# One core, attention over memories and an erf-softplus FFN: smaller TensorE bundles, one tile for both halves of the activation, a planner margin and a new order

## The chip, the cores and the metric

The kernel runs on one core of one Trainium2 chip. The metric is device time in microseconds, median over runs. Beside the runs, one execution was taken by the hardware profiler; all rows below come from that one.

## The reference

Eight batches of eight heads, 576 positions, head size 64, 32 memory slots, all in float32:

```python
a = softmax(phi, axis=positions)                # phi: B,H,576,32
k_m, v_m = a^T k, a^T v                         # 32 x 64 for each head
attn = softmax(q k_m^T / 8)                     # 576 x 32
x = concat over heads of attn v_m               # 4608 x 512
h = x w_in                                      # 512 -> 2048
out = (h * erf(softplus(h))) w_out              # 2048 -> 512
```

## The kernel before, in words

**The algebra.** Nothing is multiplied by `x`. For each batch the kernel builds `v_m w_in` ("vw", 256 rows of 32 slots by 8 heads, `vw`, L802), so the first FFN product is attention weights times vw (`psh`). Most products are made exact enough by splitting each float32 operand into a rounded half and a remainder (`hi`, `lo`) and adding three products: hi by hi, hi by lo, lo by hi (`products`, L1008). From batch 2 on the first product uses seven block products instead of eight (`ffn1_pair`, L958), on blocks that `at_blocks` (L927) makes. After it come, for each of the 128 steps (8 batches by 16 column blocks of 128), softplus and erf on ACT (L1066, L1071) and `g_split` (L1074) on DVE: `e*h` (L1097), a cast to `g_hi` (L1099), a subtraction to `g_lo` (L1100). POOL copies the last 64 positions of each half into `rest` (L1104). `ffn2` (L1114) multiplies `g_hi`, `g_lo` by the weights `wo` into four PSUM banks `pso0` to `pso3`; `ffn2_rest` (L1137) does the 64 left over positions of two batches at once into `psr`. Steps 0 to 5 use whole float32 operands (`i < FR2`).

**Small products.** Three kinds of product use only parts of the TensorE array: the sums over positions that give `k_m`, `v_m` (`sums_and_turn`, L668, tiles of 128x32, 64x32 or 116x32), the scores (`attention`, L877, 64x32, 16 matmuls) and vw (`vw`, L802, 64x32, 32 matmuls for four column blocks). They are emitted in bundles by `together` (L632). The first operation of a bundle claims every tile that the bundle writes, thus all its PSUM banks at once: two for scores, two for sums from batch 2 on, two for vw. The pool `ps` has four banks, which `psh` and `psr` use too. `PARTS` (L1282 to L1293) says which pieces go in one bundle: each batch has four vw bundles; from batch 2 on one also takes the next batch's sums, and two (in batch 2 three) also take scores of the next batch. That is 16 shared bundles of four banks each (five with sums, eleven with scores).

**The order.** Every piece of work is an `Op` with a rank (lower is earlier), a cost and the engines that may do it. `Plan.order` (L133) runs a small model of the engines once, at build time, and emits the instructions in that order. At each turn an engine takes the lowest rank among what is ready within 100 ns (L174). TensorE, when it has just run a small operation and another small one is ready, takes that one (L169). A change from large to small products is charged `SWITCH`, 98 ns, and one back `SWITCH + RELOAD`, 213 ns (L208). What an operation writes counts as ready `SIGNAL`, 60 ns, after its end (L237). The costs are in `mm`, `on_dve`, `on_act` (L349 to L356). Where TensorE would be idle for over 450 ns before the first `ffn2`, `fill` (L384) puts in matmuls of the identity. `WHEN` (L296) holds the ranks of the pieces; at the end a table (L1346) adds a number to the rank of some 400 operations, and another (L1399) fixes the engine of some 50.

**Buffers.** `AB` = 9 tiles for the attention blocks (a batch from 2 on needs 7), `WB` = 3 tiles `win`: two hold the blocks of `w_in` that `win_again` (L466) brings back from memory for one vw bundle, and `vraw`, an intermediate of `vw_sums` (L837), takes the third. `g_hi` and `g_lo` have three tiles each. SP issues nearly all DMAs.

Of the kernel before, what the change touches and what calls it, by code (L numbers as in the profile page):

```python
# [76 lines left out]
class Plan:  # L77
# [8 lines left out]
    AHEAD, WORTH = 0.0, 0.4  # L86

# [45 lines left out]
    def order(self):  # L133
# [11 lines left out]
        releases, out, now, held = [], [], 0.0, set()  # L145

# [16 lines left out]
        while len(out) < len(self.ops):  # L163
# [70 lines left out]
            for y in x.after:  # L234
                n_wait[y] -= 1
                same = e == PE and PE in y.ways
                y.ready = max(y.ready, free[PE] if same else x.end + self.SIGNAL)  # L237
                if not n_wait[y]:
                    for w in y.ways:
                        waiting[w].append(y)  # L240
            for k in x.tiles:
                if k in left:
                    left[k] -= 1
                    if not left[k]:
                        end = max(u.end for u in self.users[k]) + self.SIGNAL
                        heapq.heappush(releases, (end, len(out) * 16 + len(releases), self.pool_of[k]))
# [4 lines left out]
def tile_memory_attention_then_erf_softplus_ffn(  # L251
# [11 lines left out]
    nc = tc.nc  # L263
# [21 lines left out]
    HB, EB, AB, WB, SB, QB = 6, 5, 9, 3, 3, 0  # L285
# [10 lines left out]
    WHEN = dict(phiT=-27.5, phi=-31.75, phi_sums=-20.75, kv=-21, kv_step=-3.0, q0=-12.0, q1=-9.25, sums=-20.25, turn=-12.5, numbers=-19.0, turned=-13, part0=-3, part1=1, part2=5, part3=8.5, win=-2.25, at=-1, p0=0, p1=0.26, p2=-4.45, p3=0.31, p4=-3.9, p5=0.65, p6=-1.05, copy=-40, g=-1.25, ffn2=0.5, soft=2.05, erf=4.35, put=0, put2=1.25, vws=4.01)  # L296
# [23 lines left out]
    room.update({"g_hi": 3, "g_lo": 3, "raw": RAW, "ps": 4, "sc": SB, "dk": 1, "bias": 1, "phiT": 2, "row": 2})  # L320
# [28 lines left out]
    def mm(n, exact):  # L349
        return 2 * (2 * n / 2.4 + 2.5) if exact else n / 2.4 + (15.5 if n == DM else 11.7)  # L350
# [723 lines left out]
    def g_split(rank, i):  # L1074
# [3 lines left out]
        if i < FR2:  # L1078
            t = tile_(("g_hi", "g_lo")[i % 2], "g", i, shape=[P, S], pool="g")
            if i < IN_PSUM:  # L1080
                for x, (half, ps) in enumerate(halves_of(i)):
                    op(DVE, on_dve(U), rank, [(e, x), ps], [(t, x)],
                       lambda half=half, ps=ps: nc.vector.tensor_tensor(
                           out=get(t)[:, half], in0=get(e)[:, half], in1=get(ps)[:, :U], op=ALU.mult))
            else:
                op(DVE, on_dve(S), rank, [e, h], [t], lambda: nc.vector.tensor_tensor(
                    out=get(t), in0=get(e), in1=get(h), op=ALU.mult))
            part = [(("rest", k, x), b % 2) for x in range(2)]
            op(POOL, 400, rank, [t], part[:1], lambda: nc.gpsimd.tensor_copy(
                out=rest[:, k, 0, cols], in_=get(t)[:, NT * P :]))  # L1090
            op(POOL, 400, rank, [t, part[0]], part[1:], lambda: nc.gpsimd.tensor_tensor(
                out=rest[:, k, 1, cols], in0=get(t)[:, NT * P :],
                in1=rest[:, k, 0, cols].bitcast(F32), op=ALU.subtract))
            return
        hi = tile_("g_hi", "g_hi", i, shape=[P, S], dtype=F32R, pool="g")
        lo = tile_("g_lo", "g_lo", i, shape=[P, S], dtype=F32R, pool="g")
        op(DVE, on_dve(S), rank, [e, h], [e], lambda: nc.vector.tensor_tensor(  # L1097
            out=get(e), in0=get(e), in1=get(h), op=ALU.mult))
        op(DVE, on_dve(S, 1), rank, [e], [hi], lambda: nc.vector.tensor_copy(out=get(hi), in_=get(e)))  # L1099
        op(DVE, on_dve(S), rank, [e, hi], [lo], lambda: nc.vector.tensor_tensor(  # L1100
            out=get(lo), in0=get(e), in1=get(hi).bitcast(F32), op=ALU.subtract))
        for x, y in enumerate((hi, lo)):
            op(POOL, 400, rank, [y], [(("rest", k, x), b % 2)],
               lambda x=x, y=y: nc.gpsimd.tensor_copy(out=rest[:, k, x, cols], in_=get(y)[:, NT * P :]))  # L1104
# [9 lines left out]
    def ffn2(rank, i, d):  # L1114
# [5 lines left out]
        gs = [("g", i)] if exact else [("g_hi", i), ("g_lo", i)]  # L1120
# [6 lines left out]
        def emit():  # L1127
            w = [wf[k // 2][:, k % 2]] if exact else [get(w_key)[:, x, k % 2] for x in range(2)]
            matmuls(get(o), products([get(t)[:, d * P : (d + 1) * P] for t in gs], w), k == 0,
# [25 lines left out]
    def last_block(rank, i, gs, w_key):  # L1155
# [10 lines left out]
        for x in range(2):  # L1166
            def emit(x=x):
                matmuls(get(y[x]), products(
                    [get(g)[:, d] for g in gs], [get(w_key)[:, z, k % 2, x * n : (x + 1) * n] for z in range(2)]),
                    k == NK - TAIL, k == NK - 1)  # L1170
# [114 lines left out]
    for b in range(1, B):  # L1285
# [4 lines left out]
        for q in range(b == 1, 4):  # L1290
            PARTS.append((o + WHEN[f"part{q}"], more[q] + [(vw, b, 4 * q)]))
# [54 lines left out]
    for n, d in {  # L1346
# [139 lines left out]
```

## Time and profile before

| | |
|---|---|
| Median of the runs shown | 697.7 us (lowest 696.26) |
| The profiled execution's own time | 695.43 us |
| Its span, first to last instruction | 693.6 us |
| Instructions | 13481 |
| Moved from and to HBM | 86.50 MB read, 17.83 MB written |

The profiler lists matmuls (PE) and weight loads (PEld) apart. A matmul's listed end is modelled and runs into the next one, so the distance from start to start says what one costs, and the "busy" share of PE says little about how close it is to its best.

### The profile page before, as it was taken

To read this page: it belongs to the slowest core of one execution; us is meant where nothing else is said; L and a number is where in the kernel's file an instruction comes from. 1 tells how busy PE (TensorE), PEld (TensorE's weight loads), DVE (VectorE), ACT (ScalarE), POOL (GpSimd) and SP (SyncE) were. 2 spreads that over 40 slices of the span, in tenths; PEclk is the share of its full clock that TensorE was granted. 3 is DMA by queue.
4 is the path that set the end of the run, shared out by engine and by line. 5 is a ranking of instruction groups with operands and counts; after the bars stand their busy time and mean duration, and the time that the engine had idled before them with its cause. 6 is when DMAs were issued, how large, how long until landed. Compare 5 with 4: busy or idle time off the path is not lost.

```text
span 693.6 us, 13481 instructions
## 1 busy us (share of the span) xinstructions
PE 684.2 (99%) x5159; PEld 547.9 (79%) x5159; DVE 585.8 (84%) x1141; ACT 495.4 (71%) x813; POOL 133.4 (19%) x262
## 2 busy tenths in 40 slices
PE   8999999999999999999999999999999999999998
PEld 4566588888888877877888887888888878888886
DVE  4999999787968999999986799999976799978362
ACT  4799977979565886787674886587854677767461
POOL 0020375122102111211110123221311111211020
PEclk9999999999999999999999999999999999999999
DMA  9999950686225443354016633642112331120002
GB/s 363 416 407 402 414 188 32 198 288 188 100 80 200 174 134 120 162 191 160 1 9 241 200 69 112 243 151 108 62 47 84 91 107 61 62 92 32 0 1 76
DMA packets 29792, 105.20 MB, mean 152 GB/s; under 512 B 4000, under 2 KB 4896, under 8 KB 29728
## 3 DMA queue, kind: packets, MB, share of 16 engines
q1 hardware_dynamic: 29296, 103.27, 41.1%
q10 hardware_dynamic: 432, 1.08, 0.4%
q8 instruction: 40, 0.66, 0.4%
q14 instruction: 24, 0.20, 0.1%
HBM read 86.50 MB, written 17.83 MB: 150 GB/s over the span
## 4 chain that ended last, share of the span: by engine, by line
PE 79%; DVE 9%; ACT 5%; DMA 5%; issue 2%; SPq 0%; POOL 0%; ACTq 0%; DVEq 0%; POOLq 0%
PE pso L1109 44%; PE psh L1109 18%; PE psr L1109 6%; PE psa L794 5%; PE psh L1031 4%; PE psa L703 2%; DMA q<-qT 2%; DMA win<-w_in_away 1%; DMA out<-ot 1%; DVE g_lo L1100 1%; DVE e L1097 1%; DVE w L486 1%; DVE g_hi L1099 1%; ACT e L1066 1%; DVE h L989 1%
## 5 line engine op out<-in xcount | busy, mean ns | idle before, releaser
L1109 PE MATMUL pso<-wo,g_hi 128*128 128x512 f32 x970 | 304.9, 395 | 0.8 <-ACT ot L1186 0.8
L1109 PEld LDWEIGHTS pso<-wo,g_hi 128*128 128x128 f32 x970 | 170.3, 188 | 34.1 <-issue 6.4
L1109 PE MATMUL pso<-wo,g_lo 128*128 128x512 f32 x485 | 189.5, 391 | 0.0
L1104 POOL CAST rest<-g_hi 128x64 fp32r<-128x64 f32 x122 | 70.6, 582 | 407.4 <-DVE g_hi L1099 379.7
L1109 PE MATMUL psh<-at,vw_hi 128*128 128x288 f32 x672 | 143.4, 302 | 0.3 <-DVE h L984 0.2
L1109 PEld LDWEIGHTS psh<-at,vw_hi 128*128 128x128 f32 x672 | 113.7, 188 | 24.7 <-ACT h L985 7.1
L985 ACT ACTIVATE h<-psh 128x288 f32<-128x288 f32 x130 | 53.2, 411 | 80.3 <-PE psh L1109 79.5
L1109 PEld LDWEIGHTS pso<-wo,g_lo 128*128 128x128 f32 x485 | 91.1, 188 | 20.7 <-DVE g_lo L1100 0.2
L1097 DVE TENSOR_TENSOR e<-e,h 128x576 f32<-128x576 f32 x122 | 90.2, 752 | 11.3 <-ACT e L1071 11.0
L1066 ACT ACTIVATE e<-h 128x576 f32<-128x576 f32 x127 | 84.2, 681 | 21.4 <-DVE h L989 14.4
L1109 PE MATMUL psh<-at,vw_lo 128*128 128x288 f32 x336 | 99.2, 295 | 0.0
L1100 DVE TENSOR_TENSOR g_lo<-e,g_hi 128x576 fp32r<-128x576 f32 x122 | 92.3, 761 | 2.7
L989 DVE TENSOR_TENSOR h<-psh,h 128x288 f32<-128x288 f32 x144 | 64.0, 452 | 26.0 <-ACT h L985 14.0
L1071 ACT ACTIVATE e<-e 128x576 f32<-128x576 f32 x128 | 81.9, 679 | 0.4
L1104 POOL CAST rest<-g_lo 128x64 fp32r<-128x64 f32 x122 | 59.1, 487 | 84.7 <-DVE g_lo L1100 76.6
L1109 PEld LDWEIGHTS psh<-at,vw_lo 128*128 128x128 f32 x336 | 63.3, 188 | 0.3 <-DVE vw_lo L873 0.3
L1099 DVE CAST g_hi<-e 128x576 fp32r<-128x576 f32 x122 | 54.5, 453 | 7.9 <-PE pso L1109 7.0
L1109 PE MATMUL psr<-wo,rest 128*128 128x512 f32 x192 | 47.6, 392 | 0.0
L1071 ACT ACT_TABLE_LOAD x33 | 42.3, 1283 | 0.6
L1066 ACT ACT_TABLE_LOAD x32 | 41.1, 1283 | 0.6
L1109 PEld LDWEIGHTS psr<-wo,rest 128*128 128x128 f32 x192 | 35.3, 188 | 7.7 <-issue 0.8
L984 DVE COPY h<-psh 128x288 f32<-128x288 f32 x62 | 27.9, 450 | 7.6 <-PE psh L1109 7.2
(116 smaller groups left out, 871.9 us busy)
## 6 DMA issues: line engine op xcount, KB each, us to landing
win<-w_in_away SPq DMA_DIRECT2D x56, 512.0 KB, 5.3
kv<-kv SPq DMA_DIRECT2D x31, 640.0 KB, 7.0
q<-qT SPq DMA_DIRECT2D x16, 576.0 KB, 7.6
w<-w_in SPq DMA_DIRECT2D x8, 1023.8 KB, 14.6
w<-w_out SPq DMA_DIRECT2D x8, 1023.8 KB, 14.8
out<-ot SPq DMA_DIRECT2D x31, 256.0 KB, 2.4
w_in_away<-win SPq DMA_DIRECT2D x12, 512.0 KB, 5.4
phi<-phi SPq DMA_DIRECT2D x7, 640.0 KB, 4.7
```

What stands on the lines that cost most here:

```text
L794: nc.tensor.matmul(out=get(ps[par])[p * M : (p + 1) * M, first:n], lhsT=w[rows, p, :], rhs=x_of(rows, p), start=True, stop=True,)
L984: lambda: nc.vector.tensor_copy(out=to(), in_=get(ps[bank])),
L985: other={ACT: (on_act(U, True), lambda: nc.scalar.activation(to(), get(ps[bank]), AF.Identity))})
L989: op(DVE, on_dve(U), rank + 100 * WHEN["copy"], [ps[bank], key], [key], lambda: nc.vector.tensor_tensor(out=to(), in0=get(ps[bank]), in1=t ...
L1031: nc.tensor.matmul(out=get(ps)[:, :U], lhsT=x[:, g, k % 4 * P : (k % 4 + 1) * P], rhs=y[:, g, :], start=(n + g == 0), stop=(n == len(parts ...
L1066: last[:] = [op(ACT, on_act(S), rank, [("h", i)], [e], lambda: nc.scalar.activation(get(e), get(("h", i)), AF.Softplus), kind="softplus", ...
L1071: last[:] = [op(ACT, on_act(S), rank, [e], [e], lambda: nc.scalar.activation(get(e), get(e), AF.Erf), kind="erf", edge=edge, after=last)]
L1097: op(DVE, on_dve(S), rank, [e, h], [e], lambda: nc.vector.tensor_tensor(out=get(e), in0=get(e), in1=get(h), op=ALU.mult))
L1099: op(DVE, on_dve(S, 1), rank, [e], [hi], lambda: nc.vector.tensor_copy(out=get(hi), in_=get(e)))
L1100: op(DVE, on_dve(S), rank, [e, hi], [lo], lambda: nc.vector.tensor_tensor(out=get(lo), in0=get(e), in1=get(hi).bitcast(F32), op=ALU.subtract))
L1104: lambda x=x, y=y: nc.gpsimd.tensor_copy(out=rest[:, k, x, cols], in_=get(y)[:, NT * P :]))
L1109: nc.tensor.matmul(out=o, lhsT=y, rhs=z, start=(start and n == 0), stop=(stop and n == len(parts) - 1), skip_group_check=again,)
```

## The change

- `PARTS`: from batch 2 on, sums and scores leave the vw bundles. Each of them becomes a bundle of its own, with two banks, at the rank of the vw bundle plus `WHEN["apart"]` = -1 step. Batches 0 and 1 keep theirs.
- `g_split`: one tile `g` of [128, 2, 576] holds both halves (room 3), under two keys; steps 0 to 5 share one tile for two steps. POOL copies both halves' last 64 positions with one instruction after `lo`, in place of one each. The cast to the hi half may go to ACT, where the planner finds that earlier.
- The planner: an operation that TensorE may run counts an operand from another engine as ready `LEAD` = 120 ns later, and a buffer whose first user is on TensorE comes free 120 ns later. TensorE costs rise by 1.5 ns (512 columns) and 0.5 ns (288 columns).
- Buffers: `AB` 9 to 8, `WB` 3 to 4.
- `WHEN`, the table of rank offsets and the table of fixed engines are new throughout.

```diff
+    LEAD = 120.0
...
+        first = {p: min(self.users[ks[0]], key=self.ops.index) for p, ks in self.turn.items() if self.users[ks[0]]}
+        by_pe = {p for p, x in first.items() if PE in x.ways}
...
-                y.ready = max(y.ready, free[PE] if same else x.end + self.SIGNAL)
+                lead = self.LEAD if PE in y.ways else 0.0
+                y.ready = max(y.ready, free[PE] if same else x.end + self.SIGNAL + lead)
...
+                        end += self.LEAD if self.pool_of[k] in by_pe else 0.0
...
-    HB, EB, AB, WB, SB, QB = 6, 5, 9, 3, 3, 0
+    HB, EB, AB, WB, SB, QB = 6, 5, 8, 4, 3, 0
...
-    room.update({"g_hi": 3, "g_lo": 3, "raw": RAW, "ps": 4, "sc": SB, "dk": 1, "bias": 1, "phiT": 2, "row": 2})
+    room.update({"g": 3, "raw": RAW, "ps": 4, "sc": SB, "dk": 1, "bias": 1, "phiT": 2, "row": 2})
...
-        return 2 * (2 * n / 2.4 + 2.5) if exact else n / 2.4 + (15.5 if n == DM else 11.7)
+        return 2 * (2 * n / 2.4 + 2.5) if exact else n / 2.4 + (17.0 if n == DM else 12.2)
...
-        hi = tile_("g_hi", "g_hi", i, shape=[P, S], dtype=F32R, pool="g")
-        lo = tile_("g_lo", "g_lo", i, shape=[P, S], dtype=F32R, pool="g")
+        t = tile_("g", "g", i, shape=[P, 2, S], dtype=F32R, pool="g")
+        hi, lo = g_keys(i)
...
-        op(DVE, on_dve(S, 1), rank, [e], [hi], lambda: nc.vector.tensor_copy(out=get(hi), in_=get(e)))
+        op(DVE, on_dve(S, 1) + 65, rank, [e], [hi], lambda: nc.vector.tensor_copy(out=get(t)[:, 0], in_=get(e)),
+           other={ACT: (on_act(S), lambda: nc.scalar.activation(get(t)[:, 0], get(e), AF.Identity))})
...
-        for x, y in enumerate((hi, lo)):
-            op(POOL, 400, rank, [y], [(("rest", k, x), b % 2)],
-               lambda x=x, y=y: nc.gpsimd.tensor_copy(out=rest[:, k, x, cols], in_=get(y)[:, NT * P :]))
+        op(POOL, 600, rank, [hi, lo], [(("rest", k, x), b % 2) for x in range(2)],
+           lambda: nc.gpsimd.tensor_copy(out=rest[:, k, :, cols], in_=get(t)[:, :, NT * P :]))
+
+    def g_keys(i):
+        return [(("g", i - i % 2), i % 2)] if i < FR2 else [(("g", i), x) for x in range(2)]
...
-            PARTS.append((o + WHEN[f"part{q}"], more[q] + [(vw, b, 4 * q)]))
+            n = o + WHEN[f"part{q}"]
+            if b == 1:
+                PARTS.append((n, more[q] + [(vw, b, 4 * q)]))
+            else:
+                PARTS.append((n, [(vw, b, 4 * q)]))
+                PARTS += [(n + WHEN["apart"], [f]) for f in more[q]]
```

## Rows read from the trace of the kernel before

**Rows 1.** The page, part 1: busy us (share of the span) xinstructions.

```profile
PE 684.2 (99%) x5159; PEld 547.9 (79%) x5159; DVE 585.8 (84%) x1141; ACT 495.4 (71%) x813; POOL 133.4 (19%) x262
```

**Rows 2.** TensorE by lines, 47.5 us to the end: xcount | busy us, mean ns | idle.

```profile
L1109 PE MATMUL pso<-wo,g_hi 128*128 128x512 f32 x970 | 304.9, 395 | 0.8 <-ACT ot L1186 0.8
L1109 PE MATMUL pso<-wo,g_lo 128*128 128x512 f32 x485 | 189.5, 391 | 0.0
L1109 PE MATMUL psh<-at,vw_hi 128*128 128x288 f32 x672 | 143.4, 302 | 0.3 <-DVE h L984 0.2
L1109 PE MATMUL psh<-at,vw_lo 128*128 128x288 f32 x336 | 99.2, 295 | 0.0
L1109 PE MATMUL psr<-wo,rest 128*128 128x512 f32 x192 | 47.6, 392 | 0.0
L794 PE MATMUL psa<-win,kvm 64*32 64x256 f32 x960 | 32.9, 379 | 1.2 <-DMA win<-w_in_away 1.2
L1031 PE MATMUL psh<-at_hi,vw_hi 128*128 128x288 f32 x96 | 21.2, 303 | 0.0
...
L703 PE MATMUL psa<-kv,phi 128*32 128x128 f32 (+1 forms) x560 | 16.8, 276 | 0.5 <-ACT phi L597 0.5
L1109 PE MATMUL pso<-w,g 128*128 128x512 f32 x32 | 15.0, 602 | 0.0
```

**Rows 3.** The chain that ended last, 180 to 366 us: start us, us, what.

```profile
187.17 7.50 PE pso L1109 x33
...
300.40 1.19 PE psh L1109 x9
```

**Rows 4.** TensorE timeline, a shared bundle: start us, us, engine line op tiles xcount.

```profile
311.59 0.39 PE L1109 MATMUL pso<-wo,g_lo 128*128 128x512 f32 x1
311.91 0.71 PE L794 MATMUL psa<-q,kvm 64*32 64x288 f32 x16
312.42 1.07 PE L794 MATMUL psa<-win,kvm 64*32 64x256 f32 x32
313.42 0.73 PE L1109 MATMUL pso<-wo,g_hi 128*128 128x512 f32 x2
313.99 0.39 PE L1109 MATMUL pso<-wo,g_lo 128*128 128x512 f32 x1
```

**Rows 5.** TensorE timeline, a bundle of vw alone.

```profile
322.81 1.09 PE L794 MATMUL psa<-win,kvm 64*32 64x256 f32 x32
323.84 0.53 PE L1109 MATMUL psh<-at,vw_hi 128*128 128x288 f32 x2
```

**Rows 6.** TensorE timeline, scores alone (batch 1, first of two).

```profile
57.14 0.71 PE L794 MATMUL psa<-q,kvm 64*32 64x288 f32 x16
57.79 1.13 PE L1109 MATMUL pso<-w,g 128*128 128x512 f32 x2
```

**Rows 7.** Waits of the weight loads: us in total, times, longest us.

```profile
PEld psh L1109 <- ACT h L985: 7.1, 27, 0.5
```

**Rows 8.** Timeline at 418 us, vw waiting for its weights.

```profile
418.01 0.67 PE L794 MATMUL psa<-win,kvm 64*32 64x256 f32 x16 [0.71 <-DMA win<-w_in_away]
...
419.20 0.67 PE L794 MATMUL psa<-win,kvm 64*32 64x256 f32 x16 [0.52 <-DMA win<-w_in_away]
```

**Rows 9.** TensorE by lines, whole span: the filling matmuls.

```profile
L390 PE MATMUL idle<-ident 128*128 128x512 f32 (+3 forms) x44 | 20.8, 599 | 1.4 <-POOL ident masks.py:199 1.4
```

**Rows 10.** DVE and ACT by lines: the cast to g_hi, a whole-width activation.

```profile
L1099 DVE CAST g_hi<-e 128x576 fp32r<-128x576 f32 x122 | 54.5, 453 | 7.9 <-PE pso L1109 7.0
L1066 ACT ACTIVATE e<-h 128x576 f32<-128x576 f32 x127 | 84.2, 681 | 21.4 <-DVE h L989 14.4 <-DVE g_lo L1100 4.5 <-DVE h L1048 1.5
```

**Rows 11.** Timeline, change from batch 2 to 3: second early block, last tile, products.

```profile
242.75 0.43 ACT L941 ACTIVATE at<-f 128x288 fp32r<-128x288 f32 x1
...
268.26 1.18 DVE L943 TENSOR_TENSOR at<-f,at 128x288 fp32r<-128x288 f32 x3
...
273.06 0.53 PE L1109 MATMUL psh<-at,vw_hi 128*128 128x288 f32 x2
```

More of the change, by code (lines that the diff above doesn't have):

```diff
@@ L295, in tile_memory_attention_then_erf_softplus_ffn @@
     IN_PSUM = 1
-    WHEN = dict(phiT=-27.5, phi=-31.75, phi_sums=-20.75, kv=-21, kv_step=-3.0, q0=-12.0, q1=-9.25, sums=-20.25, turn=-12.5, numbers=-19.0, turned=-13, part0=-3, part1=1, part2=5, part3=8.5, win=-2.25, at=-1, p0=0, p1=0.26, p2=-4.45, p3=0.31, p4=-3.9, p5=0.65, p6=-1.05, copy=-40, g=-1.25, ffn2=0.5, soft=2.05, erf=4.35, put=0, put2=1.25, vws=4.01)
+    WHEN = dict(phiT=-32.0, phi=-32.75, phi_sums=-20.75, kv=-21, kv_step=-3.0, q0=-14.75, q1=-10.25, sums=-21.25, turn=-14.5, numbers=-17.25, turned=-14.25, part0=-3, part1=1, part2=5.25, part3=9.0, win=-2.25, at=-1.25, p0=0, p1=0.76, p2=-4.2, p3=0.31, p4=-1.9, p5=0.9, p6=0.95, copy=-40, g=-2.25, ffn2=0.5, soft=6.05, erf=4.35, put=-0.25, put2=1.25, vws=2.51, apart=-1)
     TAIL = 3
@@ L1078, in g_split @@
         if i < FR2:
-            t = tile_(("g_hi", "g_lo")[i % 2], "g", i, shape=[P, S], pool="g")
+            if i % 2 == 0:
+                tile_("g", "g", i, shape=[P, 2, S], pool="g")
+            t, of = g_keys(i)[0], lambda: g_of(i)[0]
             if i < IN_PSUM:
                 for x, (half, ps) in enumerate(halves_of(i)):
-                    op(DVE, on_dve(U), rank, [(e, x), ps], [(t, x)],
+                    op(DVE, on_dve(U), rank, [(e, x), ps], [t],
                        lambda half=half, ps=ps: nc.vector.tensor_tensor(
-                           out=get(t)[:, half], in0=get(e)[:, half], in1=get(ps)[:, :U], op=ALU.mult))
+                           out=of()[:, half], in0=get(e)[:, half], in1=get(ps)[:, :U], op=ALU.mult))
@@ L1085, in g_split @@
             else:
                 op(DVE, on_dve(S), rank, [e, h], [t], lambda: nc.vector.tensor_tensor(
-                    out=get(t), in0=get(e), in1=get(h), op=ALU.mult))
+                    out=of(), in0=get(e), in1=get(h), op=ALU.mult))
             part = [(("rest", k, x), b % 2) for x in range(2)]
             op(POOL, 400, rank, [t], part[:1], lambda: nc.gpsimd.tensor_copy(
-                out=rest[:, k, 0, cols], in_=get(t)[:, NT * P :]))
+                out=rest[:, k, 0, cols], in_=of()[:, NT * P :]))
@@ L1091, in g_split @@
             op(POOL, 400, rank, [t, part[0]], part[1:], lambda: nc.gpsimd.tensor_tensor(
-                out=rest[:, k, 1, cols], in0=get(t)[:, NT * P :],
+                out=rest[:, k, 1, cols], in0=of()[:, NT * P :],
                 in1=rest[:, k, 0, cols].bitcast(F32), op=ALU.subtract))
             return
-        hi = tile_("g_hi", "g_hi", i, shape=[P, S], dtype=F32R, pool="g")
-        lo = tile_("g_lo", "g_lo", i, shape=[P, S], dtype=F32R, pool="g")
+        t = tile_("g", "g", i, shape=[P, 2, S], dtype=F32R, pool="g")
@@ L1097, in g_split @@
+        hi, lo = g_keys(i)
         op(DVE, on_dve(S), rank, [e, h], [e], lambda: nc.vector.tensor_tensor(
             out=get(e), in0=get(e), in1=get(h), op=ALU.mult))
-        op(DVE, on_dve(S, 1), rank, [e], [hi], lambda: nc.vector.tensor_copy(out=get(hi), in_=get(e)))
+        op(DVE, on_dve(S, 1) + 65, rank, [e], [hi], lambda: nc.vector.tensor_copy(out=get(t)[:, 0], in_=get(e)),
+           other={ACT: (on_act(S), lambda: nc.scalar.activation(get(t)[:, 0], get(e), AF.Identity))})
         op(DVE, on_dve(S), rank, [e, hi], [lo], lambda: nc.vector.tensor_tensor(
-            out=get(lo), in0=get(e), in1=get(hi).bitcast(F32), op=ALU.subtract))
@@ L1102, in g_split @@
-        for x, y in enumerate((hi, lo)):
-            op(POOL, 400, rank, [y], [(("rest", k, x), b % 2)],
-               lambda x=x, y=y: nc.gpsimd.tensor_copy(out=rest[:, k, x, cols], in_=get(y)[:, NT * P :]))
+            out=get(t)[:, 1], in0=get(e), in1=get(t)[:, 0].bitcast(F32), op=ALU.subtract))
+        op(POOL, 600, rank, [hi, lo], [(("rest", k, x), b % 2) for x in range(2)],
+           lambda: nc.gpsimd.tensor_copy(out=rest[:, k, :, cols], in_=get(t)[:, :, NT * P :]))
+    def g_keys(i):
+        return [(("g", i - i % 2), i % 2)] if i < FR2 else [(("g", i), x) for x in range(2)]
@@ L1106, in matmuls, with g_of @@
+    def g_of(i):
+        return [get(("g", i - i % 2))[:, i % 2]] if i < FR2 else [get(("g", i))[:, x] for x in range(2)]
     def matmuls(o, parts, start, stop, again=False):
@@ L1119, in ffn2 @@
             tile_(f"pso{d}", *o)
-        gs = [("g", i)] if exact else [("g_hi", i), ("g_lo", i)]
+        gs = g_keys(i)
         w_key = raw_of[k // 2] if exact else wo[k // 2]
@@ L1128, in emit @@
             w = [wf[k // 2][:, k % 2]] if exact else [get(w_key)[:, x, k % 2] for x in range(2)]
-            matmuls(get(o), products([get(t)[:, d * P : (d + 1) * P] for t in gs], w), k == 0,
+            matmuls(get(o), products([t[:, d * P : (d + 1) * P] for t in g_of(i)], w), k == 0,
                     k == NK - 1 - TAIL * ((b, d) == (B - 1, NT - 1)))
@@ L1168, in emit @@
                 matmuls(get(y[x]), products(
-                    [get(g)[:, d] for g in gs], [get(w_key)[:, z, k % 2, x * n : (x + 1) * n] for z in range(2)]),
+                    [g[:, d] for g in g_of(i)], [get(w_key)[:, z, k % 2, x * n : (x + 1) * n] for z in range(2)]),
                     k == NK - TAIL, k == NK - 1)
@@ L1399, in tile_memory_attention_then_erf_softplus_ffn @@
     for n, e in {
-        45: ACT, 46: ACT, 104: DVE, 174: ACT, 212: ACT, 233: ACT, 326: DVE, 479: DVE, 481: ACT, 503: ACT,
-        576: DVE, 597: DVE, 710: ACT, 779: DVE, 782: ACT, 814: ACT, 850: DVE, 920: DVE, 1249: DVE, 1513: ACT,
-        1516: DVE, 1633: DVE, 1641: DVE, 1643: DVE, 1669: DVE, 1672: ACT, 1675: ACT, 1816: ACT, 1998: DVE,
-        2100: DVE, 2145: DVE, 2198: DVE, 2241: ACT, 2272: DVE, 2484: DVE, 2492: DVE, 2516: DVE, 2571: DVE,
-        2698: DVE, 2729: DVE, 2733: ACT, 2762: DVE, 2785: DVE, 2795: DVE, 2835: ACT, 2857: ACT, 2877: DVE,
-        2906: ACT, 2960: DVE, 3128: ACT,
+        210: DVE, 262: ACT, 290: DVE, 299: ACT, 301: ACT, 324: ACT, 368: ACT, 416: ACT, 420: ACT, 464: DVE,
+        473: DVE, 495: ACT, 520: ACT, 548: ACT, 615: ACT, 665: DVE, 742: DVE, 857: DVE, 902: DVE, 918: DVE,
+        989: DVE, 1064: ACT, 1072: ACT, 1113: ACT, 1120: ACT, 1164: DVE, 1176: DVE, 1256: DVE, 1280: ACT,
+        1290: ACT, 1351: ACT, 1368: DVE, 1375: DVE, 1383: ACT, 1461: DVE, 1497: ACT, 1557: DVE, 1582: DVE,
+        1619: DVE, 1622: DVE, 1673: DVE, 1711: DVE, 1787: DVE, 1825: DVE, 1876: DVE, 1956: ACT, 1972: DVE,
+        1981: ACT, 1989: ACT, 1995: ACT, 2088: ACT, 2091: ACT, 2197: ACT, 2202: ACT, 2229: ACT, 2280: DVE,
+        2363: ACT, 2437: ACT, 2447: DVE, 2511: ACT, 2604: DVE, 2635: DVE, 2689: ACT, 2737: DVE, 2741: DVE,
+        2770: DVE, 2774: ACT, 2795: ACT, 2813: DVE, 2840: ACT, 2860: ACT, 2916: ACT, 3027: DVE, 3030: DVE,
     }.items():
```

107 rows, old and new, of the table g are left out of this document.

## The prediction

> **What bounds the kernel now.** I read the page's busy shares first, then TensorE by lines, then the chain for undisturbed pitches, then the timeline around bundles, then the waits. The page says that TensorE (PE) is busy for 99% of the span, DVE for 84%, ACT for 71% [rows 1]. Since a matmul's listed end is modelled, the 99% cannot say how much of PE's time is waiting. The pitch can: 33 matmuls of 512 columns in a row take 7.50 us, 227.3 ns each, and nine of 288 columns 1.19 us, 132.2 ns each [rows 3].
>
> From 47.5 us to the end, 646.1 us, PE's own work is then worked out from the counts [rows 2]:
>
> - 512 columns, split operands: 970 + 485 + 192 = 1647 at 227.3 ns: 374.3 us
> - 288 columns: 672 + 336 + 3 x 96 (one of three equal rows stands there) = 1296 at 132.2 ns: 171.4 us
> - whole float32 operands: 32 take 15.0 us; the code has 16 more alike: 22.5 us in all
> - small products: vw 32.9, sums 16.8, and 14 lots of scores at 57.79 - 57.14 = 0.65 us [rows 6], 9.1: 58.8 us
> - the last 18 half-width matmuls, at half of 227 ns: 2 us
>
> That is 629.0 us, so waits, changes between large and small products, and the last store hold only 17 us. Before 47.5 us PE does little: 20.8 us go to filling matmuls [rows 9], put there because inputs and decoded weights are not there yet.
>
> So PE's own work is the bound. The change alters none of the counts of full-array matmuls. It can gain only from those 17 us and from the filled first stretch, and it can lose by adding changes between product kinds. To be faster by over 2% (about what a measurement of this kernel can tell from no change), 14 us, it would have to take nearly all the waiting out.
>
> **The change part by part.**
>
> *Bundles of their own.* In the shared bundle the scores begin 311.91 - 311.59 = 0.32 us after the last large matmul, 0.09 over the pitch; the bundle lasts 313.42 - 311.91 = 1.51 us; the two matmuls behind it take 0.57 us, 0.115 over two pitches [rows 4]. vw alone lasts 1.03 us [rows 5] and scores alone 0.65 [rows 6], together 1.68, or 0.17 more than shared. A split that stands apart therefore costs 0.17 + 0.09 + 0.115 = 0.375 us of PE. Sums I price alike. There are 16 of them: 6.0 us if every one stands apart, nothing where the planner runs the two back to back, which it does when the second is ready as the first ends. A gain in this term itself is excluded, since no small product goes away. With the scores ranked one step ahead they often will be apart, but new rank offsets may undo that; I take six of 16, +2.25 us. What it buys is room: two PSUM banks are claimed at a time, not all four, so the pool need not be empty before a bundle. The trace shows no long wait ahead of the bundle above (0.09 us), so the room buys less waiting behind it at most.
>
> The Trainium skill has a rule that speaks against this edit. In "TensorEngine Tiling (Array Packing)", section "Tiling Modes", key properties, it says that changing the tiling mode, not just the tile, drains TensorE. The trace agrees in kind: the change in and out costs the 0.09 and 0.115 us above. By the rule alone every separate bundle pays, the 6.0 us; by the row it is paid only where a large matmul comes between.
>
> *Margin for TensorE's operands.* Weight loads for the first product waited 27 times for ACT's copy out of `psh`, 7.1 us in total [rows 7], 0.26 us each. Part of that is hidden by the matmul under way. Of the 17 us about 6 to 7 are changes into and out of some thirty bundles at 0.205 us; the other 10 hold the last store too, and I count 7 of them as waits. A planner that counts operands as ready later puts other work in front of such a product. Ends: all 7 gone, or as many new ones since the whole order is new, +7; I take a third, -2.5 us. It costs nothing where `ffn2` work lies ready, and six steps of lag keep some.
>
> *Fourth `win` buffer.* One vw bundle waited for its weights, 0.71 and 0.52 us of idle PE [rows 8]. Two blocks and `vraw` fill the three buffers, so the next blocks start late. The fourth lets one block of the two start earlier. Ends 0 and -1.2; I take -1.0, as the new order also moves the loads. It is part of the 7.
>
> *One tile `g`, one POOL copy, cast on either engine.* POOL loses 122 instructions at 19% busy [rows 1], off every long wait of PE; its copy now waits for `lo`, but `rest` is needed only for `psr`, a batch later. The cast takes DVE 453 ns, and ACT's pass of the same width 681 ns [rows 10]: a cast that moves frees 0.45 us of DVE and takes 0.68 us of ACT, which is 29% idle. The cover is PE's lag; DVE is not the bound, so I take 0. If that cover were gone, ten casts on the wrong engine would cost 10 x (0.68 - 0.45) = 2.3 us, or gain as much.
>
> *`AB` 8.* A new batch uses seven blocks; with nine tiles two are made early, the second at 242.75 us in batch 3, with eight only one. It moves into the stretch that ends at 268.26 + 1.18 = 269.44 us; the first product comes at 273.06 [rows 11], 3.6 us later. One block more, ACT's 0.43 us and a DVE subtraction of a third of 1.18, 0.39, fits: 0. Without the slack it is 0.82 us for each of five changes of batch, +4.1.
>
> *The new order, first 47.5 us.* The first loads keep their places: each pool hands out its tiles in the code's order. Behind them the work on DVE and ACT is free to move. Of the 20.8 us of filling I take a tenth, -2 us; no row sets the sign, so +4 to -5.
>
> *Sum.* +2.25 - 2.5 - 1.0 + 0 + 0 - 2 = -3.25 us on the profiled execution's 695.43: 692.2. That execution lies 2.3 us under the median shown, 697.7. The same offset gives 694.5 us.
>
> **The rivals.**
>
> *The drains decide* (slower than before). All 16 bundles stand apart, +6.0 us, and the waits are merely moved: 701.4, with the offset 703.7. For it: a shift by a whole step, far above the 1.51 us that a bundle lasts [rows 4]. Against: the planner charges 0.31 us for each round trip, near the 0.375 measured, so it has reason to join them. It decides from the point where ten or more stand apart (3.75 us) and the other terms bring less than 3.75. By the Trainium skill's rule on tiling modes ("TensorEngine Tiling (Array Packing)", "Tiling Modes") this is the outcome.
>
> *The waits all go and the start shortens.* -6 of waits, -4 of filling, +1 for three separate bundles: 686.4, with the offset 688.7. For it: the margin aims at just the wait that stands 27 times in the list [rows 7]. Against: the waits are already short (0.5 us at most), and each is a choice among what is ready, so that a margin moves some and brings others.
>
> *Batch changes starve* (`AB` 8): +4.1 and +2.25, nothing gained elsewhere: 701.8, with the offset 704.1. Against: 3.6 us of slack [rows 11].
>
> *The parts cancel.* The splits cost what the waits bring and the start stays: 695.4, with the offset 697.7.
>
> **How the numbers follow.** Forecast (691 to 697 us) 0.45; cancel 0.15; drains 0.18; waits and start 0.15; batch changes 0.04; beyond all of these 0.03. The range 687 to 703 us leaves out the far halves of the drains case and a few of the rest, about 2 in 10. Two per cent is 683.7 and 711.7: faster 0.04, which needs more than all the waits; slower 0.03, which needs the drains, the batch changes and a worse start together; same 0.93.
>
> **What would show it.** Right: the counts of 512- and 288-column matmuls unchanged; between six and ten separate scores or sums bundles, each about 0.2 us of PE in changes; the 27 waits of the loads for ACT's copies down to under 15; no idle PE on `win`; POOL with about 122 instructions fewer; filling near 19 us. Wrong: `psa` bundles all apart with PE's sum up by 6 us; a wait for `at` tiles at a batch change; DVE or ACT chains that leave PE without `ffn2` work; a first stretch longer than 47.5 us before the first float32 `pso` product.

## The result and the profile after

The changed kernel takes 688.57 us (median of 4 runs, 687.73 to 689.58), the kernel before 696.26 us beside it on the same chip: ratio 0.9886, 95% interval 0.986 to 0.9912. (The medians of the kernel before, of s_lead0 and of s2_ctrl leave out one stray run each, of 1119.66, 1850.92 and 1346.44 us; the 697.7 us shown ahead of the prediction still count the first.) That is some 8 us less, in the forecast direction and inside the range of 687 to 703 us, but below the 691 to 697 us that the forecast held likeliest, and more than twice the 3.25 us of the sum. The profiled execution after takes 689.58 us with a span of 687.8 us; the one before took 695.43. The two traces lie 5.85 us apart, less than the medians, because the one before was quicker than every run beside it (695.71 us at best) and the one after is the slowest of its four.

Part 1 of the page after answers to [rows 1]:

```profile
PE 676.7 (98%) x5153; PEld 547.8 (80%) x5153; DVE 570.7 (83%) x1089; ACT 531.7 (77%) x869; POOL 76.5 (11%) x140
```

TensorE is as full as before. POOL lost 122 instructions. DVE lost 52 and ACT won 56: that is mainly the cast to the hi half, which the planner gave to ACT 72 times out of 122. Of the copies out of `psh` 15 went the other way (115 on ACT, 130 before). DVE and ACT by lines after (count, busy us, mean ns, idle before), against [rows 10]:

```profile
L1106 DVE CAST g<-e 128x576 fp32r<-128x576 f32 x50 | 22.8, 459 | 8.8 <-PE pso L1122 8.3
L1107 ACT ACTIVATE g<-e 128x576 fp32r<-128x576 f32 x72 | 49.1, 683 | 30.3 <-PE pso L1122 23.9 <-DVE e L1104 3.2 <-issue 2.9
```

TensorE by lines after, from 47.5 us on, against [rows 2]:

```profile
L1122 PE MATMUL pso<-wo,g 128*128 128x512 f32 x1455 | 373.9, 394 | 3.4 <-DVE wo L384 2.1 <-ACT ot L1199 1.0
L1122 PE MATMUL psh<-at,vw_hi 128*128 128x288 f32 x672 | 140.4, 297 | 1.0 <-ACT h L990 0.9
L1122 PE MATMUL psh<-at,vw_lo 128*128 128x288 f32 x336 | 98.8, 294 | 0.0
L1122 PE MATMUL psr<-wo,rest 128*128 128x512 f32 x192 | 47.0, 390 | 0.0
L799 PE MATMUL psa<-win,kvm 64*32 64x256 f32 x960 | 32.7, 381 | 0.0
```

The counts are unchanged: 1455 + 192 = 1647 of 512 columns, and the same 672 and 336. `psa<-win` waits for nothing any more. `pso` now idles 3.4 us and not 0.8: 2.1 of them, for DVE's lo half of `wo`, are new, and 1.0 is for ACT's copy to `ot`; both come back below. The waits of the weight loads after (us in total, times, longest us), against [rows 7]:

```profile
PEld pso L1122 <- DVE wo L384: 2.8, 2, 1.5
PEld psh L1122 <- DVE h L989: 1.9, 5, 0.5
PEld pso L1122 <- ACT ot L1199: 1.8, 2, 1.4
PEld psh L1122 <- ACT h L990: 1.1, 1, 1.1
```

The 27 waits of `psh` for ACT's copies out of `psh` have become one. Those for DVE's copies, which now number 77 and not 62, are 5 and were 7 before:

```profile
PEld psh L1109 <- DVE h L984: 2.5, 7, 0.6
```

The filling matmuls, against [rows 9], and the first `ffn2` product, before (L1109) and after (L1122):

```profile
L395 PE MATMUL idle<-ident 128*128 128x512 f32 (+3 forms) x38 | 16.7, 559 | 1.4 <-POOL ident masks.py:199 1.4
```

```profile
50.50 1.98 PE L1109 MATMUL pso<-w,g 128*128 128x512 f32 x4
...
39.93 4.82 PE L1122 MATMUL pso<-w,g 128*128 128x512 f32 x10
```

Where the time went can be read by asking in both traces when the same amount of TensorE's own work (each matmul at its pitch) had started. The figures are us from the start of the span:

```
own work done    20      50      60     300     480     630
before         48.9    80.4    90.5   340.3   526.6   680.2
after          44.2    75.9    89.4   337.1   522.4   674.3
difference     -4.8    -4.5    -1.1    -3.3    -4.2    -5.9
```

The kernel after wins 4.8 us before 49 us, gives back 3.7 of them before 91 us (the two waits for `wo`, 1.20 and 1.49 us beyond the pitch, are most of it), and wins another 4.8 little by little. Summing from the trace all starts that came more than 30 ns after the pitch, from 89 us on and without those behind a small product, gives 14.6 us in 130 places before and 10.6 us in 85 after. Starts of `psh` make 3.4 of these 4.1 us: 6.9 us in 70 places before, 3.4 in 26 after.

### The profile page after: what moved, and what is told of

Same layout as the page of the kernel before. It is cut to its first block, busy times and chain, and to the rows that moved or that the text cites. A ratio compares the mean times of both kernels' runs of the same rounds, so it can differ in the third digit from the quotient of the medians.

```text
span 687.8 us, 13246 instructions
## 1 busy us (share of the span) xinstructions
PE 676.7 (98%) x5153; PEld 547.8 (80%) x5153; DVE 570.7 (83%) x1089; ACT 531.7 (77%) x869; POOL 76.5 (11%) x140
## 3 DMA queue, kind: packets, MB, share of 16 engines
q10 hardware_dynamic: 432, 1.08, 0.4%
## 4 chain that ended last, share of the span: by engine, by line
PE 87%; ACT 5%; DMA 4%; DVE 3%; issue 1%; SPq 0%; ACTq 0%
PE pso L1122 49%; PE psh L1122 19%; PE psr L1122 6%; PE psa L799 6%; PE psh L1036 5%; PE psa L708 2%; DMA q<-qT 2%; DMA out<-ot 2%; ACT w L488 1%; ACT e L1071 1%; DMA phiT<-phiT 1%; ACT h L1054 0%; DVE e L1104 0%; ACT L1076 0%; DVE wo L384 0%
## 5 line engine op out<-in xcount | busy, mean ns | idle before, releaser
L1122 PE MATMUL pso<-wo,g 128*128 128x512 f32 x1455 | 373.9, 394 | 3.4 <-DVE wo L384 2.1
L1122 PEld LDWEIGHTS pso<-wo,g 128*128 128x128 f32 x1455 | 260.4, 188 | 57.8 <-issue 8.4
L1122 PE MATMUL psh<-at,vw_hi 128*128 128x288 f32 x672 | 140.4, 297 | 1.0 <-ACT h L990 0.9
L1122 PEld LDWEIGHTS psh<-at,vw_hi 128*128 128x128 f32 x672 | 116.7, 188 | 19.7 <-DVE h L989 1.9
L1111 POOL CAST rest<-g 128x128 fp32r<-128x128 f32 x122 | 69.0, 571 | 548.6 <-DVE g L1108 509.1
L1122 PE MATMUL psh<-at,vw_lo 128*128 128x288 f32 x336 | 98.8, 294 | 0.0
L1108 DVE TENSOR_TENSOR g<-e,g 128x576 fp32r<-128x576 f32 x122 | 90.3, 751 | 6.2 <-ACT g L1107 5.5
L990 ACT ACTIVATE h<-psh 128x288 f32<-128x288 f32 x115 | 46.9, 408 | 53.2 <-PE psh L1122 52.6
L1107 ACT ACTIVATE g<-e 128x576 fp32r<-128x576 f32 x72 | 49.1, 683 | 30.3 <-PE pso L1122 23.9
L1122 PEld LDWEIGHTS psh<-at,vw_lo 128*128 128x128 f32 x336 | 63.4, 189 | 0.0
L989 DVE COPY h<-psh 128x288 f32<-128x288 f32 x77 | 34.7, 451 | 17.0 <-PE psh L1122 16.6
L1122 PE MATMUL psr<-wo,rest 128*128 128x512 f32 x192 | 47.0, 390 | 0.0
L1122 PEld LDWEIGHTS psr<-wo,rest 128*128 128x128 f32 x192 | 35.4, 188 | 7.0 <-issue 0.2
L871 DVE TENSOR_TENSOR vw_lo<-psa,vw_hi 128x512 fp32r<-128x512 f32 x48 | 31.7, 679 | 2.0 <-ACT vw_hi L865 1.7
L799 PE MATMUL psa<-win,kvm 64*32 64x256 f32 x960 | 32.7, 381 | 0.0
L859 DVE TENSOR_TENSOR vraw<-psa,vraw 128x256 f32<-128x256 f32 x72 | 28.9, 414 | 2.8 <-ACT vw_hi L865 2.2
## 6 DMA issues: line engine op xcount, KB each, us to landing
w<-w_in SPq DMA_DIRECT2D x8, 1023.8 KB, 14.6
```

The lines of the kernel that those rows point to most:

```text
L799: nc.tensor.matmul(out=get(ps[par])[p * M : (p + 1) * M, first:n], lhsT=w[rows, p, :], rhs=x_of(rows, p), start=True, stop=True,)
L989: lambda: nc.vector.tensor_copy(out=to(), in_=get(ps[bank])),
L990: other={ACT: (on_act(U, True), lambda: nc.scalar.activation(to(), get(ps[bank]), AF.Identity))})
L1107: other={ACT: (on_act(S), lambda: nc.scalar.activation(get(t)[:, 0], get(e), AF.Identity))})
L1111: lambda: nc.gpsimd.tensor_copy(out=rest[:, k, :, cols], in_=get(t)[:, :, NT * P :]))
L1122: nc.tensor.matmul(out=o, lhsT=y, rhs=z, start=(start and n == 0), stop=(stop and n == len(parts) - 1), skip_group_check=again,)
```

## Experiments

In the kernels whose name begins with f_ the changed kernel's order is written out as a list and only the entries named are moved, so that all else stays in place. Those beginning with s_ or s2_ got an order by a search of their own on the kernel's planner; "planner's end" is the end of the plan in its own model.

**Yardstick.** The changed kernel once more:

> The changed kernel again, as the yardstick of this group. Both theories: 0.986 to 0.991 of the kernel before, and a profile with one psh weight load waiting for ACT's copy (the first profile had 1.1 us in 1) and with 14 of 16 scores or sums bundles run back to back with vw.

Measured 689.26 us (688.61 to 692.24), ratio 0.9898 [0.9869, 0.9928]. Its trace, a second one of the changed kernel, has the same span of 687.8 us but not the same waits. At 60 us of own work nothing is left of the gain of the start: three waits of 1.0 to 1.2 us between 76 and 80 us, for DVE's `win` and for ACT's and DVE's `wo`, and a slower clock behind them (last section) took it. In return the copy to `ot` at 300 us waits for nothing. So single waits of about 1 us can come and go from one execution to the next; the short late starts of `psh` (0.03 to 0.3 us, from 89 us on) do not: 2.3 us in 25 places in the first trace, 2.3 in 24 in the second, against 6.5 in 69 before.

**First products right behind their copies** (f_tight). An example of the 22 moves, on TensorE's list:

```diff
-799 871 872 802 804
+799 871 802 872 804
```

> The changed kernel's order written out as it stands, but 22 first-product matmul groups go ahead of the large ffn2 group in front of them, so that by the planner's reckoning they start within 120 ns of their operands (0.3 us of waiting in all by its own figures). Theory A, the margin is what took the waits away: each such start costs about 0.2 us on the chip (0.1 of wait, 0.1 of the second weight load late), 22 x 0.2 = 4.4 us over the yardstick, and psh weight loads wait some 20 times. Rival B, the waits went with the new order's other freedoms and the planner's 60 ns was right: 0 to 0.5 us.

Measured 692.27 us (690.96 to 692.63), 0.9927 [0.9901, 0.9953]: 3.0 us over the yardstick, by its median and by its span alike. The intervals of the two ratios overlap, but seven of the changed kernel's eight runs lie below all four of these. The weight loads' waits in that run:

```profile
PEld psh L1122 <- DVE h L989: 5.3, 18, 0.5
PEld psh L1122 <- ACT h L990: 3.4, 7, 1.6
```

From 6 waits of 3.0 us to 25 of 8.7. The short late starts of `psh` rose from 2.3 us in 24 places to 4.2 in 42; the rest of the 3.0 us is in single waits, above all one at 389 us that was there already and grew from 0.87 to 1.56. So a product that starts as its operand arrives costs between 1.9 / 22 = 0.09 us, by the short starts alone, and 3.0 / 22 = 0.14, less than the theory's 0.2, and far from the rival's nothing. This is what the margin avoids.

**Bundles kept apart** (f_apart). One `ffn2` group between the two bundles of each of 14 pairs, for example:

```diff
-683 719 695 657 682
+683 719 657 695 682
```

> The changed kernel's order written out, with one ffn2 group moved between the two bundles of each of the 14 pairs that run back to back. By the prediction's price: about nine pairs of scores at 0.375 us and five with sums at 0.2 to 0.375, 4.4 to 5.2 us over the yardstick. Rival: changes between small and large products hide behind other work, under 1 us.

Measured 697.87 us, 1.0018 [1.0004, 1.0031]: 8.6 us over the yardstick, 0.61 us for each pair. Both theories were too low. A pair that was pulled apart, on TensorE's timeline of that run:

```profile
306.68 0.86 PE L1122 MATMUL pso<-wo,g 128*128 128x512 f32 x3
307.46 0.72 PE L799 MATMUL psa<-q,kvm 64*32 64x288 f32 x16
308.11 0.96 PE L1122 MATMUL pso<-wo,g 128*128 128x512 f32 x3
309.00 1.09 PE L799 MATMUL psa<-win,kvm 64*32 64x256 f32 x32
```

Three products of 512 columns take 0.682 us at their pitch [rows 3]; here 0.78 pass before the scores and 0.89 between the two bundles. The drain itself is thus about what the forecast read. The other 0.2 us per pair is not in these rows. It fits that everything behind comes at another moment: `psh` starts late by 5.4 us in 46 places (3.2 in 25 in the yardstick's trace), and single waits of 1.08, 0.73 and 0.62 us came up that the yardstick does not have. The Trainium skill's rule that a change of tiling mode drains TensorE ("TensorEngine Tiling (Array Packing)", "Tiling Modes") agrees with these rows. By that rule scores and vw, both with tiles of 64x32, change no mode between them, and such a pair lasts 1.51 us whichever goes first; the prediction let every separate bundle pay by the rule, which is more than the rule says.

**All casts on DVE, same order** (f_casts_dve). One of the 72, on ACT's list and DVE's:

```diff
-ACT 305 318 350 319
+ACT 305 318 319
-DVE 304 306 367 248
+DVE 304 306 350 367 248
```

> The changed kernel's order written out, with the 72 casts to the hi half that ACT does given to DVE at the same places. Adds 72 x 0.453 = 33 us to DVE (570.7 to about 603 us busy) and takes 49 from ACT. If TensorE's lag covers it, as predicted: within 1 us of the yardstick. Rival, the way to ACT is what keeps DVE in time: 5 us or more over the yardstick, with waits of psh or pso for DVE.

Measured 699.96 us, 1.0046 [1.0032, 1.0059]: 10.7 us over the yardstick. DVE is busy for 594.1 us, and the loads wait 6.5 us in 13 and 3.0 in 9 for its work on `h`. Taken alone, that would make the cast the whole gain. But this order was made for casts on ACT, so the next runs gave other versions orders of their own.

**Three searched orders** (s_dve, s_lead0, s_joined): all casts on DVE; `LEAD` 0; scores and sums (x) bound to a vw bundle (y) again.

```diff
-           other={ACT: (on_act(S), lambda: nc.scalar.activation(get(t)[:, 0], get(e), AF.Identity))})
...
-    LEAD = 120.0
+    LEAD = 0.0
...
+            x.before |= y.before - {x}
+            x.placed += [t for t in y.placed if t not in x.placed]
+            x.rank, y.rank, y.follows = y.rank, y.rank + 1e-3, x
```

> The changed kernel with all 122 casts on DVE again (72 had gone to ACT), and this time an order searched for that: ranks and engines of everything else were moved until the planner's own end stood at 683.8 us, against 680.2 for the changed kernel. The yardstick is the changed kernel's 689.3 us of the first call, 9.1 over its planner's end. Theory A, the choice of engine carries a good part of the gain whatever the order: 692.9 us (683.8 + 9.1) or more, DVE near 590 us busy, waits of TensorE's loads for DVE's copies out of psh over 5 us. Rival, the 10.7 us of the earlier run with casts on DVE came from an order that was made for the other engine, and the choice itself is worth nothing: 689.3 to 690.5 us.

> The changed kernel with a margin of 0 in the planner, in an order searched for that (planner's end 680.6 us, so it would lose only 0.5 by the plan). Theory A, a product that starts just as its operand arrives costs TensorE about 0.14 us, as the run with 22 moved groups showed: some 46 first products stand so tight again, 46 x 0.14 = 6.4 us, 689.3 + 0.5 + 6.4 = 696 us, at least 693; waits of the loads for copies out of psh from 3 us in 6 to over 7 us in 20 or more. Rival, the margin is bookkeeping, and what counts is the plan's end: 689.8 us, within 1 of the changed kernel.

> The changed kernel with scores and sums joined again to a vw bundle (all four banks claimed before the first product, the second bundle bound to follow), in an order searched for that (planner's end 682.4 us). Theory A, the split pays by the room that two banks at a time leave: the plan's 2.2 us show on the chip, 691.5 us. Rival, 14 of 16 pairs ran back to back anyway, so that joining them changes nothing but the two that stood apart: 688.5 to 689.5 us.

Measured 697.4 us (1.0012 [0.9981, 1.0044]), 701.73 us (1.0053 [1.0033, 1.0072]) and 700.6 us (1.0066 [1.004, 1.0092]). As times these settle nothing on the three parts. All lie 4 us or more above every time that the theories named, though the first two theories A gave only a least value (692.9 and 693 us) and so are not refuted. The search had also moved work in the first 100 us (20 us of own work are done 1.4 to 4.3 us later than in the changed kernel), the clock fell in every run of s_lead0 and s_joined (mean granted clock 0.990 to 0.998), and there was no control. One thing can be read off. The loads' waits in the run without margin:

```profile
PEld psh L1122 <- ACT h L990: 5.3, 22, 0.3
PEld psh L1122 <- DVE h L989: 3.4, 12, 0.4
```

34 waits of 8.7 us for the copies, as before the change (27 of 7.1 us for ACT's [rows 7] and 7 of 2.5 for DVE's). The short late starts of `psh` are back too, 7.6 us in 81 places.

**The same with a control** (s2_ctrl, s2_dve, s2_joined). The first 100 us are the changed kernel's, instruction by instruction; behind them the ranks are shaken and searched again, each for the same time. The control changes nothing else:

> A control for the searched orders: the changed kernel with nothing changed but its order. The first 100 us and the loads' ranks are those of the changed kernel; behind them every rank was shaken and then searched again in the same way and for as long as in the two runs beside this one. Planner's end 682.3 us, 2.1 over the changed kernel's own. If a searched order does on the chip what the plan says: 689 + 2.1 = 691 us. Rival, an order that was never run on the chip holds waits that the plan does not know (loads and stores that queue behind one another), and the earlier searched runs lost most of their time to these: 696 us or more. Whichever it is, it is the yardstick for the next two.

> Like the control, but all casts behind 100 us on DVE (117 of 122). Planner's end 683.8 us, 1.5 over the control's. Theory A, DVE's load itself makes TensorE wait: 4 us or more over the control, with more waits of the loads for DVE's copies out of psh. Rival, a fitting order hides nearly all of it, as the forecast had it: the plan's 1.5 us over the control, or less.

> Like the control, but scores and sums joined to a vw bundle again, four banks claimed at once. Planner's end 684.0 us, 1.7 over the control's, though it has seven changes of product kind fewer (74 against 88 in the plan, two make one round trip of some 0.375 us, 2.6 us). Theory A, two banks at a time leave room that is worth more than the changes: the plan's 1.7 us over the control or more, with larger waits ahead of the bundles. Rival, the split brings nothing: the control's time or up to 3 us less.

Measured: control 696.53 us, 1.0001 [0.9989, 1.0013]; casts on DVE 698.64 us, 1.0032 [1.0016, 1.0048]; joined 700.12 us, 1.0059 [1.004, 1.0078].

The control is the most telling run. It has every part of the change and stands exactly at the time of the kernel before: an order that is 2.1 us worse in the plan is 7 us worse on the chip. Its loads wait little for copies out of `psh` (2.1 us in 7 for DVE's, 0.7 in 3 for ACT's), so the margin works there too. From 89 us on its trace starts products late by 5.6 us more than the first trace of the changed kernel, in three parts of nearly the same size. Waits of 0.3 us and more hold 1.6 of them, the changes between large and small products 1.9, and short late starts 2.1, of which `psh` has 1.6 (3.9 us in 40 places, not 2.3 in 25). Of the long waits these three, among TensorE's waits in the control, are new or longer:

```profile
PE pso L1122 <- ACT ot L1199: 1.3, 3, 0.8
PE psh L1036 <- ACT kvk L753: 1.0, 1, 1.0
...
PE psa L708 <- DMA kv<-kv: 0.6, 1, 0.6
```

The changes are ten more in its plan (88 against 78), five round trips. Against this control the cast on ACT is worth 698.64 - 696.53 = 2.1 us, near the plan's 1.5 and below theory A's 4: its rival, the forecast's view, comes closer. The run waits 3.0 us for `ot` copies where the control waits 1.3, so about 2 us is rather an upper end; the runs at a mean granted clock of 0.999 or more lie 1.6 us apart (697.93 and 696.34 us).

The joined run is 3.6 us over the control, as theory A had it, but that settles nothing. At the same amount of own work it is 1.3 us ahead of the control at 180 us; one vw bundle at 253 us then waits 2.13 us for its weights and 0.88 more for their second block, the clock falls behind it (last section), and 3.0 us behind is where it ends. The fall of the clock is not the whole of it: one run with a mean granted clock of 1.0 took 699.45 us. Whether the four banks claimed at once brought that wait, or this one order did, stays open.

**Stores ahead of loads** (f_stores). After the change two copies to `ot` waited for their tile. On ACT's timeline after:

```profile
300.13 0.60 ACT L1199 ACTIVATE ot<-pso 128x512 f32<-128x512 f32 x1 [1.37 <-DMA out<-ot]
...
388.51 0.60 ACT L1199 ACTIVATE ot<-pso 128x512 f32<-128x512 f32 x1 [2.21 <-DMA out<-ot]
```

On SP's timeline after, the store that frees the tile is issued behind two loads of `win`:

```profile
291.71 0.34 SPq L1202 DMA_DIRECT2D out<-ot  x1
292.10 1.94 SPq L474 DMA_DIRECT2D win<-w_in_away  x2
294.09 2.12 SPq L1202 DMA_DIRECT2D out<-ot  x2
```

The edit moves the loads behind it, on SP's list at 292 us and at 379 us:

```diff
-1356 1381 1391 1359 1362
+1356 1359 1381 1391 1362
...
-1768 1899 1796 1806 1771 1774 1777
+1768 1771 1774 1899 1796 1806 1777
```

> The changed kernel, same order, but two loads of win at 292 us go out behind the store of the second output tile and three loads at 379 to 380 us behind two stores, not ahead of them. Theory A, the copies of pso that waited for their tile (1.37 and 2.21 us) waited for a store queued behind these loads, and TensorE lost 1.14 and 1.06 us to it: both waits go, 687.3 us. Rival, the stores take as long anyway or the late loads make vw wait: 689 to 690 us.

Measured 687.59 us (686.95 to 688.4), 0.9861 [0.9842, 0.9881]. ACT's copies at the two places, in that run:

```profile
298.39 0.58 ACT L1199 ACTIVATE ot<-pso 128x512 f32<-128x512 f32 x1
...
386.54 0.59 ACT L1199 ACTIVATE ot<-pso 128x512 f32<-128x512 f32 x1
```

No wait is left at either. The two stores that had been queued behind loads now take 2.16 and 2.03 us from issue to landing; in the first trace they took 5.94 and 5.76. At the same amount of TensorE's own work the run is 0.6 us ahead of that trace up to 240, 1.8 at 270 and 3.0 from 360 on: two steps of 1.2 us, where the waits were. Against the yardstick's trace only the second step is there, of 1.0 us, since there the store at 295 us took 5.00 us and nothing waited for it. So the edit is worth 1 us in one comparison and 2.4 in the other. By the medians the gain is 1 to 1.7 us, and the intervals of the ratios overlap. It is the fastest version measured here.

**Weights split earlier as well** (f_both). On top of that, on ACT's list and DVE's (282 and 325 make hi halves of `wo`, 283 and 326 lo halves):

```diff
-ACT 316 243 282 317
+ACT 316 282 243 317
-ACT 319 284 320 325
+ACT 319 325 284 320
-DVE 268 244 245 246 283
+DVE 268 283 244 245 246
-DVE 351 285 404 326
+DVE 351 326 285 404
```

> The version with the stores ahead of the loads (687.6 us in the second call, 1.4 to 2 under the changed kernel), and two pairs of splits of wo made earlier: ACT's hi half of the fourth and fifth weight pair and DVE's lo half of each go ahead of decoding and softmax steps that nothing waits for so soon. Theory A, TensorE's waits for DVE at 77 and 84 us (1.2 and 1.5 us beyond the pitch) were only a matter of order: both go, 685 us, no wait of pso for wo over 0.3 us. Rival, DVE is busy without a gap from 65 to 85 us, so that the 2.4 us of work moved ahead make something else late: 687 to 688 us.

Measured 690.44 us, 0.9919 [0.9894, 0.9943]: 2.9 us worse than without it by the medians, 3.8 by the spans of the two traces. TensorE's waits in that run:

```profile
PE psh L1036 <- DVE sc L897: 1.8, 1, 1.8
...
PE psh L1036 <- ACT vw_hi L382: 1.1, 1, 1.1
...
PE pso L1122 <- DVE wo L384: 0.7, 1, 0.7
```

The 2.1 us of waits for `wo` shrank to 0.7, and 2.9 us for other work of DVE and ACT came up in their place, as the rival said, at a higher price than it gave. Behind the longest of them, at 94 us, the clock was granted at 0.50 from 95.2 to 98.5 us; at half speed that is another 1.7 us, nearly half of the loss. This one order only chose anew who waits for DVE and ACT; that no order could do better is not shown.

## Why the prediction was right or wrong

**The bound** was right: TensorE's own work is unchanged, and all that moved is waiting, changes of kind and the first stretch. That 2% is about what a measurement can tell from no change was too coarse: the interval here reaches 0.26% to either side.

**Bundles, +2.25 us.** Six of 16 were to stand apart; two do, at 201.83 and 225.85 us, 0.75 us by the forecast's price. The other 14 run back to back with a vw bundle. In four of the five with sums vw now goes first, and the pair lasts 3.29 us, not 3.13, 0.65 us together. So the cost is about 1.4 us, and the planner did join them because each round trip is charged, as the text on the first rival had it. That rival's condition (ten apart) did not come, but its price was too low: at the 0.61 us measured, 16 apart would have cost 9.8 us, not 6.0. What the room of two banks bought stays open, as the joined run ended on one long wait.

**Margin, -2.5 us.** This term was mis-sized. The forecast took a third of 7 us because a margin "moves some and brings others". The waits for copies fell from 27 to one for ACT's, and all late starts of `psh` behind 89 us from 6.9 to 3.4 us, although 1.06 of that is a new wait that has nothing to do with the margin (below). Leaving that wait aside, these starts gained 4.5 us. The run that took 22 of them back lost 3.0. Not all of the 4.5 is the margin's: the control has the same margin in another order, and there the short late starts came down from 6.5 us to 3.9 and not to 2.3, a gain of 2.6.

**Fourth `win` buffer, -1.0 us.** The waits are gone [rows 8]; by the late start and the stretched bundle they had cost 0.98 + 0.76 = 1.7 us. A new order moved the loads at the same time, and the buffer alone was not tried. It does not suffice by itself: in s2_joined and s_joined, which have four buffers too, vw waited for its weights again, 2.13 and 2.06 us at the longest.

**Cast on either engine, 0.** The term was put at nothing and measured about 2 us in favour of the change: 2.1 against the control. The bound of 2.3 us had been worked out for ten casts; 72 moved. The 10.7 us of the first attempt were an order that no longer fitted. POOL's single copy and `AB` 8 were not tried alone; the trace shows no wait for `rest` or for an `at` tile.

**First 47.5 us, -2 us.** The start gained 4.8 us, near the bound of 5, as the first `ffn2` product starts at 39.93 us and not at 50.50. But the forecast stopped its account there. By 91 us only 1.1 us were left, and none in the yardstick's trace: the earlier the products run, the sooner they want `wo`, and the one try to split it sooner made other work late.

**What was not in the sum.** Two `ot` copies that waited for a store cost 2.2 us in the first trace after, and one cost 0.87 in the second; before, two such waits cost 0.67 and 0.45. And the forecast gave the new order no price of its own behind 47.5 us except inside the margin's ends. The control shows what hangs on it: 7 us, with all parts kept.

**The time and the second rival.** The measured 688.57 us is not the forecast's 694.5 but the 688.7 of the rival "the waits all go and the start shortens", which had 0.15. Most of its signs came: waits down by 4.5 and 1.7 us, filling down by 4.1 us (20.8 to 16.7), two bundles apart and not three. But its start did not last beyond 91 us, and by the traces the change brought 5.85 us, about midway between the forecast's 3.25 and the rival's 9. That its median was met so closely is luck in part: its 2.3 us between profiled execution and median start from the 697.7 us; from 697.0, the middle of the other two runs shown, they are 1.6.

Adding the measured terms: +1.4 - 4.5 - 1.7 - 1.1 + 1.1 = -4.8 of the 5.85 us between the traces; the remaining 1 us is spread over many starts. The step that went wrong is the size of the margin's term, and behind it the treatment of an order as the sum of its parts.

## What to carry to other kernels

When a change comes with a new order of the whole program, price the parts from rows, but widen the range by what an order alone can do; here that was 7 us with nothing else changed. Judge a part by a control whose order was made in the same way, not by swapping the part under an order made for another. And where a few long waits remain, look at the queue behind which the releasing transfer was issued: moving five loads behind three stores took two of them away, at no cost that the trace shows.

## What the runs showed of the hardware

A pause of TensorE of some 2 us could cost its own length again. In s_joined a vw bundle waited 2.06 us beyond the pitch at 255 us, and in these windows (us, busy us of PE, PEld, DVE, ACT and POOL, granted clock, DMA share, GB/s) the clock was granted at 0.50, which is 1.2 GHz and not 2.4, for the 5 us from 259.5 on (it had fallen at 258.1):

```profile
245.00:255.00 10.00, 10.00 (x92) 7.90 (x91) 9.97 (x21) 8.20 (x14) 0.59 (x2) 1.00 0.46 64
255.00:259.50 4.50, 2.07 (x35) 0.54 (x33) 4.48 (x8) 3.37 (x5) 0.98 (x2) 0.85 0.75 279
259.50:264.50 5.00, 5.00 (x19) 3.80 (x12) 0.64 (x2) 2.17 (x5) 0.00 (x0) 0.50 0.56 201
264.50:270.00 5.50, 5.50 (x34) 5.01 (x33) 4.45 (x10) 4.41 (x12) 0.00 (x0) 0.96 0.00 0
```

Twelve products of 512 columns take 5.29 us there, 0.44 each, against 0.227 [rows 3]. s_dve (a wait of 2.23 us at 397 us, then 0.52 for 3.5 us) and s2_joined (2.13 us at 253 us, then 0.50 for 3 us) show the same, and so does f_both (1.96 us at 94 us, then 0.50 from 95.2 to 98.5 us); s2_dve, which waited 2.05 us at 304 us, kept 1.00. No single wait of 1 to 1.5 us in the first trace after the change did this, but three close together did: in the yardstick's trace TensorE waited 1.15, 1.01 and 1.20 us between 76 and 80 us, and then stood at 0.50:

```profile
76.00:80.50 4.50, 2.09 (x35) 0.80 (x20) 4.01 (x6) 4.46 (x6) 0.00 (x0) 1.00 1.04 423
80.60:83.90 3.30, 3.30 (x11) 2.73 (x10) 3.30 (x7) 3.30 (x6) 0.00 (x0) 0.50 1.00 416
```

This spreads the times of one and the same kernel: of the yardstick's four runs the two with a mean granted clock of 1.0 took 688.61 and 688.91 us, the one with 0.995 took 692.24.

The other surprise is the price of a tight start. By the plan the 22 moved products cost 0.3 us in all; on the chip they cost 3.0. What in TensorE takes these 0.09 to 0.14 us each, the rows do not say.
